# Attention, then an MLP: the first two batches read k in blocks of permuted rows, and each output tile gets a PSUM tile of its own

## The chip, the cores and the metric

The kernel runs on one core of one Trainium2 chip. The metric is the device time of one execution in microseconds (us). The engines are TensorE (PE), VectorE (DVE), ScalarE (ACT), GpSimd (POOL) and SyncE (SP); PE's weight loads have a row of their own (PEld). Loads of q, k and v are issued by SP, loads of the weights and nearly all stores by POOL.

## The reference

Eight batches, eight heads, 576 tokens, head size 64. Each token sees itself and the 127 tokens before it, with a bias that falls linearly with the distance; then each token (512 features) goes through an MLP with a swish.

```
scores = (q @ k.T) / sqrt(64) - slope[h] * |i - j|      # only 0 <= i - j < 128
x = softmax(scores) @ v                                 # to [4608, 512]
h = x @ w_in                                            # 512 -> 2048
out = (h * sigmoid(beta * h)) @ w_out                   # 2048 -> 512
```

## The kernel before

Everything that PE multiplies is bfloat16. The 4,608 tokens of the MLP are cut into nine groups of 512. For a group g, `HS(g, j)` (`Hm`) makes one of 16 slices of the hidden layer: four matmuls into one of two PSUM tiles `hps` (L436), a tanh on ACT (L443), a product on DVE into `gT` (L444). `OS(g, i, n)` is a quarter of the 16 matmuls of one output tile of 128 tokens (L457); after the last quarter ACT scales the tile from PSUM to SBUF (`osb`, L463), and `store` issues its DMA (L470). The output tile is one half of `OO`, a single PSUM tile of two banks; i % 2 picks the half.

Attention of batches 0 and 1 goes by pairs of heads p, with 512 of the 576 tokens. `get_pair` loads q and k so that partition r holds rows 4r to 4r+3; `cast_pair` (POOL, L203) makes bfloat16 of them; `TP` transposes them on PE, and one DVE copy (L233) writes q and k to `QK`, back in the order of the rows. `SP_` makes scores: first a matmul of the identity with `table`, the bias and mask of each head, then q and k on top of it (L275). Visit A goes to `SS`, visit B to `OO`. ACT takes the exponential (L281); `PVP` multiplies by v (L304) and norms on DVE; `XP` transposes the result, and a DVE copy writes it to `XT` (L316). The last 64 tokens of a batch follow in a tail: `TT`, `SCT` (with `tablet` for a bias), `PV`, `X`. Batches 2 to 7 transpose by DMA (`DT`) and mask after the exponential (`SC`, L364 to L378; all in `SS`).

The order of PE, SP and POOL is the order of the program throughout; ACT and DVE keep it too in the opening. The opening is batch 0: constants, its four pairs, then `constants_late` (copies into `tablet`, clearing, all on DVE but one identity), `betas`, and the first two H steps. Then H steps 2 to 15 of group 0 run with the list `second` between them, which holds batch 1's four pairs and the tail of batch 0. Group 1 begins with H steps alone, and then H steps and output steps alternate; `spread` puts the steps of batches 2 to 7 (`att`), whose loads and casts are in `jobs`, between the items of all later groups. The loads of batch 1 wait for the second quarter of w_in.

The pool `fst` of loaded tiles has 13 buffers, `bst` of cast ones four; `psum_t` (transposes, `pv`, `xt`) and `psum_h` have two each.

Of the kernel before, what the change touches and what calls it, by code (L numbers as in the profile page):

```python
# [19 lines left out]
def kernel(  # L20
# [62 lines left out]
    SS = psum_c.tile([P, 2, 512], F32, name="SS")  # L83
    OO = psum_c.tile([P, 2, 512], F32, name="OO")
    psum_c.seal()

    def after(ins, other):
# [7 lines left out]

    def tri(o, n, w, sign, base, cm):
        nc.gpsimd.affine_select(
            out=o, in_=o, pattern=[[sign, w]], base=base, channel_multiplier=cm,
            compare_op=ALU.is_ge, fill=FAR,
        )  # L100

    def constants():
        nc.vector.memset(warm[:], 0.0)
        nc.scalar.activation(out=warm[:], in_=warm[:], func=ACTF.Exp)
        nc.gpsimd.iota(
            rel[:, 0:2, :], pattern=[[P, 2], [1, P]], base=0, channel_multiplier=-1,
            allow_small_or_imprecise_dtypes=True,
        )
        tri(rel[:, 0], 1, P, 1, 0, -1)
        tri(rel[:, 1], 1, P, -1, -1, 1)  # L110
        make_identity(nc, ident[:])
        nc.vector.tensor_copy(out=rel[:, 2], in_=rel[:, 0])
        for h in range(H):
            nc.vector.tensor_scalar_mul(table[:, h], rel[:], -slopes[h] / qscale)
        for i in range(2):
            nc.vector.memset(VS[i][:, :, :, D : D + 1], 1.0)

    def constants_late():
        make_identity(nc, identf[:])
        for e in range(2):  # L120
            for p in range(NP):
                for a in range(2):
                    nc.vector.tensor_copy(
                        out=tablet[:, e, a, p], in_=table[:, 2 * p + e, a, 0:64])
        for i in range(2):
            nc.vector.memset(VS[i][64:P, 4, :, 0:D], 0.0)
            nc.vector.memset(QK[i][:, :, :, S:], 0.0)
        nc.vector.memset(PC[:, 1024:], 0.0)
# [41 lines left out]

    def get(what, b, sb):
# [55 lines left out]
    def TP(b, p):  # L227
        src = staged.pop((b, "p", p))
        tps = psum_t.tile([P, 2, 4, P], BF16, name="tps", tag="t")
        for i in range(2):  # L230
            for c in range(4):
                nc.tensor.transpose(out=tps[:, i, c], in_=src[:, i, c], identity=ident[:])  # L232
        nc.vector.tensor_copy(  # L233
            out=QK[b % 2][:, :, p, 0:FULL].rearrange("d i (r c) -> d i c r", c=4), in_=tps[:])

# [17 lines left out]
    def SP_(b, vis, p):  # L253
        qk = QK[b % 2]
        sps = SS if vis == "A" else OO
        w = WIDTH[vis]
# [10 lines left out]
        for kb, at, q0, n in VISIT[vis]:  # L267
            for e in range(2):
# [261 lines left out]
    with tc.manual_schedule(engines={ENG.PE, ENG.SP, ENG.Pool}):  # L530
        with tc.manual_schedule(engines={ENG.Activation, ENG.DVE}):
            for w in ("p0", "p1", "v0", "v1", "p2", "p3", "v2", "v3"):
                n = int(w[1])
                if w[0] == "p":
                    get_pair("q", 0, n)
                    get_pair("k", 0, n)
                else:
                    get("v", 0, n)
            nc.sync.dma_start(out=bflat[:], in_=moe_beta.rearrange("(j p) -> j p", p=P))
            constants()  # L540
            w1 = []
            cast_pair(0, 0)
# [107 lines left out]
        items += o[8:]  # L650
        done, dw, dj = 0, 0, 0
# [70 lines left out]
```

## Time and profile before

| | us |
|---|---|
| median of three runs | 387.45 |
| lowest and highest | 383.09, 389.43 |
| the profiled execution | 388.25 |
| its span in the trace | 386.5 |
| PE busy | 338.2 |
| DVE busy | 214.1 |
| ACT busy | 206.9 |
| POOL busy | 102.9 |

The span is the time between the first and the last instruction of the trace. Matmuls are pipelined, so a busy PE is not PE at its peak: the same matmul of 512 columns takes twice as long where the granted clock is half. The mean granted clock of the run was 0.956 of full.

### The profile page before, as it was taken

To read this page: it belongs to the slowest core of one execution; us is meant where nothing else is said; L and a number is where in the kernel's file an instruction comes from. 1 tells how busy PE (TensorE), PEld (TensorE's weight loads), DVE (VectorE), ACT (ScalarE), POOL (GpSimd) and SP (SyncE) were. 2 spreads that over 40 slices of the span, in tenths; PEclk is the share of its full clock that TensorE was granted. 3 is DMA by queue.
4 is the path that set the end of the run, shared out by engine and by line. 5 is a ranking of instruction groups with operands and counts; after the bars stand their busy time and mean duration, and the time that the engine had idled before them with its cause. 6 is when DMAs were issued, how large, how long until landed. Compare 5 with 4: busy or idle time off the path is not lost.

```text
span 386.5 us, 6289 instructions
## 1 busy us (share of the span) xinstructions
PE 338.2 (87%) x2357; PEld 158.6 (41%) x2357; DVE 214.1 (55%) x454; ACT 206.9 (54%) x392; POOL 102.9 (27%) x188
## 2 busy tenths in 40 slices
PE   3676868699879999989999989999999899999985
PEld 1343334334334444434444434444444445444432
DVE  6567488636344478636646672875387536525400
ACT  2331445344575678646757764676677645426411
POOL 5838134100244444340224403331200100010010
PEclk9765799969989999999999999999999999999999
DMA  8999999692059999994866794793100010010021
GB/s 210 196 254 236 187 197 200 105 206 39 27 117 209 228 221 211 204 220 91 170 132 141 154 203 104 165 168 76 56 0 30 27 56 27 30 54 26 3 81 54
DMA packets 136126, 49.44 MB, mean 128 GB/s; under 512 B 125456, under 2 KB 133664, under 8 KB 136096
## 3 DMA queue, kind: packets, MB, share of 16 engines
q1 hardware_dynamic: 129152, 35.93, 49.6%
q0 software_dynamic: 6944, 13.11, 13.2%
q8 instruction: 18, 0.29, 0.3%
q14 instruction: 12, 0.10, 0.1%
HBM read 36.71 MB, written 9.44 MB: 119 GB/s over the span
## 4 chain that ended last, share of the span: by engine, by line
PE 71%; DVE 14%; ACT 11%; issue 3%; DMA 1%; POOL 0%; ACTq 0%
PE OO L457 30%; PE hps L436 28%; ACT pt L374 6%; DVE qkT L233 5%; PE SS L364 3%; DVE gT L444 3%; ACT osb L463 3%; DVE pt L378 2%; ACT sig L443 2%; PE xt L414 1%; PE pv L403 1%; PE pv L399 1%; PE tps L232 1%; PE pv L304 1%; DVE xnp L289 1%
## 5 line engine op out<-in xcount | busy, mean ns | idle before, releaser
L436 PE MATMUL hps<-XT,W 128*128 128x512 bf16 x576 | 149.8, 392 | 7.9 <-DVE gT L444 5.1
L457 PE MATMUL OO<-W,gT 128*128 128x512 bf16 x576 | 143.7, 381 | 11.5 <-ACT osb L463 11.4
L443 ACT ACTIVATE sig<-hps,beta_h 128x512 bf16<-128x512 f32 x144 | 98.6, 690 | 81.3 <-PE hps L436 78.5
L444 DVE SCALAR_TENSOR_TENSOR gT<-sig,hps 128x512 bf16<-128x512 bf16 x144 | 97.6, 684 | 70.7 <-ACT sig L443 70.0
L374 ACT ACTIVATE pt<-SS,bias 128x256 bf16<-128x256 f32 (+1 forms) x192 | 75.0, 477 | 21.2 <-PE SS L364 21.2
L436 PEld LDWEIGHTS <-W 128*128 128x128 bf16 x576 | 53.5, 100 | 70.2 <-issue 20.9
L457 PEld LDWEIGHTS <-gT 128*128 128x128 bf16 x576 | 52.6, 98 | 70.4 <-issue 16.6
L470 POOL DMA_DIRECT2D out_dram<-osb x34 | 18.4, 542 | 214.1 <-ACT osb L463 214.1
L463 ACT ACTIVATE osb<-OO 128x512 f32<-128x512 f32 x36 | 21.7, 604 | 47.1 <-PE OO L457 45.5
L378 DVE TENSOR_TENSOR pt<-pt,mask 128x1024 bf16<-128x1024 bf16 x48 | 35.8, 746 | 17.1 <-ACT pt L374 17.0
L288 DVE RECIPROCAL zs<-pv 128x4 f32<-128x4 f32 (+1 forms) x80 | 13.8, 176 | 31.2 <-PE pv L403 24.5
L196 POOL CAST bst<-fst 128x512 bf16<-128x512 f32 (+1 forms) x32 | 21.2, 661 | 30.2 <-PE tps L232 16.9
L209 POOL CAST vs<-fst 128x512 bf16<-128x512 f32 (+1 forms) x40 | 24.7, 629 | 13.0 <-DMA fst<-in_v_dram 8.9
L289 DVE TENSOR_TENSOR xn<-pv,zs 128x256 bf16<-128x256 f32 (+1 forms) x64 | 26.8, 421 | 1.6
L420 DVE COPY XT<-xt 128x512 bf16<-128x512 bf16 (+1 forms) x32 | 12.3, 385 | 19.6 <-PE xt L414 19.3
L233 DVE COPY qkT<-tps 128x1024 bf16<-128x1024 bf16 x8 | 19.5, 2434 | 6.5 <-PE tps L232 6.5
L364 PE MATMUL SS<-qkT 64*128 64x256 bf16 (+2 forms) x240 | 19.4, 256 | 3.3 <-ACT pt L374 3.3
L197 POOL CAST bst<-fst 128x512 bf16<-128x512 f32 (+1 forms) x32 | 19.7, 615 | 3.8 <-DMA fst<-in_k_dram 3.7
L403 PE MATMUL pv<-vs,pt 128*128 128x65 bf16 x240 | 20.6, 193 | 0.0
L403 PEld LDWEIGHTS <-pt 128*128 128x128 bf16 x240 | 16.1, 97 | 6.7
L364 PEld LDWEIGHTS <-qkT 64*128 64x128 bf16 x240 | 8.2, 94 | 22.6 <-issue 22.1
L399 PE MATMUL pv<-vs,pt 128*128 128x65 bf16 x192 | 17.4, 193 | 0.0
(62 smaller groups left out, 159.6 us busy)
## 6 DMA issues: line engine op xcount, KB each, us to landing
out_dram<-osb POOLq DMA_DIRECT2D x34, 256.0 KB, 2.3
fst<-in_q_dram SPq DMA_DIRECT2D x32, 256.0 KB, 5.1
fst<-in_k_dram SPq DMA_DIRECT2D x32, 256.0 KB, 5.0
fst<-in_v_dram SPq DMA_DIRECT2D x32, 256.0 KB, 4.0
W<-in_moe_w_in_dram POOLq DMA_DIRECT2D x4, 512.0 KB, 6.8
W<-in_moe_w_out_dram POOLq DMA_DIRECT2D x4, 512.0 KB, 9.8
fst<-in_q_dram SPq DMA_DIRECT2D x8, 128.0 KB, 3.8
fst<-in_k_dram SPq DMA_DIRECT2D x8, 128.0 KB, 4.1
```

Source lines behind the costliest of these rows:

```text
L209: return nc.gpsimd.tensor_copy(out=VS[b % 2][0:rows, sb, :, 0:D], in_=fs.pop(("v", b, sb))[0:rows])
L233: nc.vector.tensor_copy(out=QK[b % 2][:, :, p, 0:FULL].rearrange("d i (r c) -> d i c r", c=4), in_=tps[:])
L289: nc.vector.tensor_tensor(out=xn, in0=pv[0:nq, :, 0:D], in1=zs[0:nq].broadcast_to([nq, 4, D]), op=ALU.mult)
L364: nc.tensor.matmul(o, lhsT=qk[64 * e : 64 * e + 64, 1, p, P * kb : P * kb + P], rhs=qk[64 * e : 64 * e + 64, 0, p, P * kb : P * kb + nq], ...
L374: nc.scalar.activation(out=pt[:, e, cols], in_=sps[:, e, cols], func=ACTF.Exp, scale=qscale, bias=bias[:, half, h : h + 1],)
L378: nc.vector.tensor_tensor(out=pt[:], in0=pt[:], in1=masks[m][:], op=ALU.mult)
L403: nc.tensor.matmul(pv[:, hl, 0 : D + 1], lhsT=weights(b, qb, h, 0), rhs=vs[:, qb, h, 0 : D + 1], start=qb == 0, stop=True,)
L436: nc.tensor.matmul(hps[:], lhsT=W1[:, c, bass.ts(j, P)], rhs=XT[:, c, c0 : c0 + TOKG], start=(c == 0), stop=(c == NDM - 1),)
L443: nc.scalar.activation(out=sig[:], in_=hps[:], func=ACTF.Tanh, scale=beta_h[:, j : j + 1])
L444: nc.vector.scalar_tensor_tensor(out=gts[g][:, j, :], in0=sig[:], scalar=1.0, in1=hps[:], op0=ALU.add, op1=ALU.mult)
L457: nc.tensor.matmul(ops_, lhsT=gT[:, j, i * P : i * P + P], rhs=W2[:, j, :], start=(j == 0), stop=(j == NFF - 1),)
L463: nc.scalar.mul(osb[:], ops_, 0.5)
```

## The change

It has seven parts.

- For batches 0 and 1 DVE copies q from PSUM as the transposes leave it (all rows of one residue c together), and k in blocks: within each 128 keys the 32 keys of residue 0 come first, then those of residue 1, and so on. `SP_` therefore reads q with a step of 128 elements, four at a time, so that queries come out in their own order. Two copies take the place of one.
- The distance table of those keys is built by four iotas on 32 partitions each, one iota over columns and five DVE operations, in place of one iota and two selects on POOL.
- v of batches 0 and 1 has to have the same order of keys: four DMAs to 32 partitions each take the place of one. v 0 and 1 of batch 0 are issued by ACT, after the constants.
- Eight matmuls of zeros stand ahead of the first transposes on PE.
- What `constants_late` did on DVE goes to POOL; the first half of `tablet` comes from a small table `relt` of its own. The identity for `betas` is made after it.
- Visit B of batches 0 and 1 gets its own PSUM tile `SX`; after batch 1 its banks are given to a pool `psum_o` of two single tiles, and each output tile is one of these.
- The list `second` is spread over the H steps from 4 on, where it was from 9 on; in group 1 four H steps stand ahead of the first output step, where there were eight.

```
 def constants():
+    nc.vector.memset(zeros[:], 0.0)
...
+    for _ in range(8):
+        nc.tensor.matmul(SS[:, 0, :], lhsT=zeros[:, 0:P], rhs=zeros[:], start=True, stop=True,
+            skip_group_check=True)
+    for c in range(4):
+        nc.gpsimd.iota(ktok[32 * c : 32 * c + 32], pattern=[[0, 1]], base=c, channel_multiplier=4, ...)
-    nc.gpsimd.iota(rel[:, 0:2, :], pattern=[[P, 2], [1, P]], base=0, channel_multiplier=-1, ...)
-    tri(rel[:, 0], 1, P, 1, 0, -1)
-    tri(rel[:, 1], 1, P, -1, -1, 1)
+    nc.gpsimd.iota(qtok[:], pattern=[[1, P]], base=0, channel_multiplier=0, ...)
     make_identity(nc, ident[:])
+    nc.vector.tensor_scalar(out=qtok[:], in0=qtok[:], scalar1=ktok[:, 0:1], scalar2=None, op0=ALU.subtract)
+    for a, cmp in ((0, ALU.is_lt), (1, ALU.is_ge)):
+        nc.vector.tensor_scalar(out=pen[:], in0=qtok[:], scalar1=0.0, scalar2=FAR, op0=cmp, op1=ALU.mult)
+        nc.vector.scalar_tensor_tensor(out=rel[:, a], in0=qtok[:], scalar=float(P * a), in1=pen[:],
+            op0=ALU.add, op1=ALU.add)
     nc.vector.tensor_copy(out=rel[:, 2], in_=rel[:, 0])
...
 def constants_late():
-    make_identity(nc, identf[:])
-    (16 nc.vector.tensor_copy to tablet; 5 nc.vector.memset)
+    nc.gpsimd.iota(relt[:], ...)
+    nc.gpsimd.affine_select(out=relt[:], in_=relt[:], ...)
+    nc.gpsimd.tensor_copy(out=tablet[:, :, 1], in_=table[:, :, 1, 0:64].rearrange("k (p e) t -> k e p t", e=2))
+    for h in range(H):
+        nc.gpsimd.tensor_scalar_mul(tablet[:, h % 2, 0, h // 2], relt[:], -slopes[h] / qscale)
+    (the same 5 memsets, on nc.gpsimd)
 def betas():
+    make_identity(nc, identf[:])
...
 def get(what, b, sb, eng=None):
+    if what == "v" and b < 2 and sb < 4:
+        for c in range(4):
+            (eng or nc.sync).dma_start(
+                out=f[32 * c : 32 * c + 32],
+                in_=src[b, :, P * sb : P * sb + P, :].rearrange("h (r c) d -> c r h d", c=4)[c])
+        return
...
 def TP(b, p):
-    nc.vector.tensor_copy(
-        out=QK[b % 2][:, :, p, 0:FULL].rearrange("d i (r c) -> d i c r", c=4), in_=tps[:])
+    nc.vector.tensor_copy(
+        out=qk[:, 0, p, 0:FULL], in_=tps[:, 0].rearrange("d c r -> d (c r)"))
+    nc.vector.tensor_copy(
+        out=qk[:, 1, p, 0:FULL].rearrange("d (n c r) -> d c n r", n=4, c=4),
+        in_=tps[:, 1].rearrange("d c (n r) -> d c n r", n=4))
...
 def SP_(b, vis, p):
-    sps = SS if vis == "A" else OO
+    sps = SS if vis == "A" else SX
...
-        rhs=qk[64 * e : 64 * e + 64, 0, p, q0 : q0 + n],
+        rhs=qk[64 * e : 64 * e + 64, 0, p, 0:FULL].rearrange(
+            "d (c r) -> d r c", c=4)[:, q0 // 4 : (q0 + n) // 4, :],
...
 def OS(g, i, n):
-    ops_ = OO[:, i % 2, :]
+    if n == 0:
+        late[g, i] = late["o"].tile([P, DM], F32, name="ops", tag="ops")
+    ops_ = late[g, i][:]
...
-            else:
+            elif n >= 2:
                 get("v", 0, n)
...
         constants()
+        for n in range(2):
+            get("v", 0, n, nc.scalar)
...
-        to = len(second) * (j + 1 - 9) // (NFF - 9)
+        to = len(second) * max(0, j + 1 - 4) // (NFF - 4)
...
+    opening.close()
+    late["o"] = ctx.enter_context(tc.tile_pool(name="psum_o", bufs=2, space=bass.MemoryType.PSUM))
...
-    items = h[:8]
+    items = h[:4]
-    for n in range(8):
-        items += [h[8 + n]] + o[n : n + 1]
+    for n in range(12):
+        items += [h[4 + n]] + o[n : n + 1]
```

## Rows read from the trace of the kernel before

**Rows 1.** The page: busy time by engine; the chain that ended last, by line.

```profile
PE 338.2 (87%) x2357; PEld 158.6 (41%) x2357; DVE 214.1 (55%) x454; ACT 206.9 (54%) x392; POOL 102.9 (27%) x188
PE OO L457 30%; PE hps L436 28%; ACT pt L374 6%; DVE qkT L233 5%; PE SS L364 3%; DVE gT L444 3%; ACT osb L463 3%; DVE pt L378 2%; ACT sig L443 2%; PE xt L414 1%; PE pv L403 1%; PE pv L399 1%; PE tps L232 1%; PE pv L304 1%; DVE xnp L289 1%
```

**Rows 2.** Groups by line and shape, 0 to 60 us: count | busy us, mean ns | idle.

```profile
L233 DVE COPY qkT<-tps 128x1024 bf16<-128x1024 bf16 x7 | 17.0, 2431 | 6.5 <-PE tps L232 6.5
...
L316 DVE COPY XT<-xt 128x512 bf16<-128x512 bf16 x4 | 1.7, 417 | 0.2 <-PE xt L315 0.2
...
L112 DVE COPY rel<-rel 128x128 f32<-128x128 f32 x1 | 0.4, 448 | 0.7 <-POOL rel L97 0.7
```

**Rows 3.** What PE waited for, whole span: us in total, times, longest.

```profile
PE OO L457 <- ACT osb L463: 11.4, 17, 1.2
PE SS L275 <- DVE qkT L233: 10.5, 6, 2.2
...
PE hps L436 <- DVE XT L316: 2.0, 1, 2.0
...
PE pv L304 <- DVE qkT L233: 0.8, 1, 0.8
```

**Rows 4.** Stretches: length, busy us by engine (instructions), granted clock, DMA share, GB/s.

```profile
10.00:20.00 10.00, 6.20 (x56) 3.34 (x56) 5.54 (x5) 3.37 (x4) 8.62 (x19) 0.77 1.04 195
20.00:30.00 10.00, 7.27 (x74) 4.26 (x73) 6.86 (x29) 3.15 (x4) 3.63 (x14) 0.67 1.20 257
30.00:40.00 10.00, 6.52 (x32) 3.00 (x30) 7.04 (x30) 1.26 (x2) 8.76 (x14) 0.50 1.09 229
```

**Rows 5.** Timeline, H steps alone: start, us, engine, operation, count, idle before.

```profile
46.61 1.99 PE L436 MATMUL hps<-XT,W 128*128 128x512 bf16 x8 [0.53 <-DVE gT L444]
...
77.72 3.57 PE L436 MATMUL hps<-XT,W 128*128 128x512 bf16 x8 [0.38 <-DVE XT L420]
```

**Rows 6.** Timeline of the opening's first 15 us.

```profile
6.07 2.43 DVE L233 COPY qkT<-tps 128x1024 bf16<-128x1024 bf16 x1 [0.81 <-PE tps L232]
...
9.10 0.81 ACT L281 ACTIVATE pt<-SS 128x768 bf16<-128x768 f32 x1 [6.80 <-PE SS L275]
...
13.67 0.61 POOL L203 CAST bst<-fst 128x512 bf16<-128x512 f32 x1 [0.19 <-DMA fst<-in_k_dram]
...
14.86 0.40 PE L275 MATMUL OO<-qkT 64*128 64x128 bf16 x6
15.19 0.38 PE L304 MATMUL pv<-vs,pt 128*128 128x65 bf16 x6
```

**Rows 7.** Timeline, 15 to 37 us: the end of the opening.

```profile
15.92 2.25 POOL L216 DMA_DIRECT2D W<-in_moe_w_in_dram  x3
...
28.28 0.61 POOL L203 CAST bst<-fst 128x512 bf16<-128x512 f32 x1 [5.97 <-DMA fst<-in_q_dram]
...
32.21 2.78 DVE L123 COPY tablet<-table 128x64 bf16<-128x64 bf16 x16
...
36.94 1.01 PE L436 MATMUL hps<-XT,W 128*128 128x512 bf16 x2 [2.01 <-DVE XT L316]
```

**Rows 8.** Timeline, batch 1: the first scores behind the copy.

```profile
53.12 0.34 PE L275 MATMUL SS<-qkT 64*128 64x256 bf16 x4 [2.19 <-DVE qkT L233]
```

**Rows 9.** PE's waits from 100 to 365 us, and the tail's timeline.

```profile
PE OO L457 <- ACT osb L463: 8.6, 13, 1.2
PE SS L364 <- ACT pt L374: 3.3, 3, 1.9
...
370.18 3.61 PE L457 MATMUL OO<-W,gT 128*128 128x512 bf16 x16 [0.69 <-ACT osb L463]
```

**Rows 10.** SP's timeline: DMA issues.

```profile
0.81 0.44 SPq L187 DMA_DIRECT2D fst<-in_q_dram  x1
...
2.83 1.41 SPq L177 DMA_DIRECT2D fst<-in_v_dram  x2
4.28 2.66 SPq L187 DMA_DIRECT2D fst<-in_q_dram  x1
```

More of the change, by code (lines that the diff above doesn't have):

```diff
@@ L58 @@
     one = const.tile([P, 1], BF16, name="one")
+    ktok = const.tile([P, 1], F32, name="ktok")
+    qtok = const.tile([P, P], F32, name="qtok")
+    pen = const.tile([P, P], F32, name="pen")
     rel = const.tile([P, 3, P], F32, name="rel")
+    relt = const.tile([P, 64], F32, name="relt")
+    zeros = const.tile([P, 512], BF16, name="zeros")
     table = const.tile([P, H, 3, P], BF16, name="table")
@@ L83 @@
     SS = psum_c.tile([P, 2, 512], F32, name="SS")
-    OO = psum_c.tile([P, 2, 512], F32, name="OO")
     psum_c.seal()
+    opening = ExitStack()
+    psum_x = opening.enter_context(tc.tile_pool(name="psum_x", bufs=1, space=bass.MemoryType.PSUM))
+    SX = psum_x.tile([P, 2, 512], F32, name="SX")
+    late = {}
     def after(ins, other):
@@ L92, in after @@
         )
[L96 to L100, printed above, removed]
     def constants():
+        nc.vector.memset(zeros[:], 0.0)
         nc.vector.memset(warm[:], 0.0)
         nc.scalar.activation(out=warm[:], in_=warm[:], func=ACTF.Exp)
+        for _ in range(8):
+            nc.tensor.matmul(
+                SS[:, 0, :], lhsT=zeros[:, 0:P], rhs=zeros[:], start=True, stop=True,
+                skip_group_check=True)
+        for c in range(4):
+            nc.gpsimd.iota(
+                ktok[32 * c : 32 * c + 32], pattern=[[0, 1]], base=c, channel_multiplier=4,
+                allow_small_or_imprecise_dtypes=True,
+            )
         nc.gpsimd.iota(
-            rel[:, 0:2, :], pattern=[[P, 2], [1, P]], base=0, channel_multiplier=-1,
+            qtok[:], pattern=[[1, P]], base=0, channel_multiplier=0,
             allow_small_or_imprecise_dtypes=True,
         )
-        tri(rel[:, 0], 1, P, 1, 0, -1)
-        tri(rel[:, 1], 1, P, -1, -1, 1)
         make_identity(nc, ident[:])
+        nc.vector.tensor_scalar(
+            out=qtok[:], in0=qtok[:], scalar1=ktok[:, 0:1], scalar2=None, op0=ALU.subtract)
+        for a, cmp in ((0, ALU.is_lt), (1, ALU.is_ge)):
+            nc.vector.tensor_scalar(
+                out=pen[:], in0=qtok[:], scalar1=0.0, scalar2=FAR, op0=cmp, op1=ALU.mult)
+            nc.vector.scalar_tensor_tensor(
+                out=rel[:, a], in0=qtok[:], scalar=float(P * a), in1=pen[:], op0=ALU.add,
+                op1=ALU.add)
         nc.vector.tensor_copy(out=rel[:, 2], in_=rel[:, 0])
@@ L118, in constants_late @@
     def constants_late():
-        make_identity(nc, identf[:])
-        for e in range(2):
-            for p in range(NP):
-                for a in range(2):
-                    nc.vector.tensor_copy(
-                        out=tablet[:, e, a, p], in_=table[:, 2 * p + e, a, 0:64])
+        nc.gpsimd.iota(
+            relt[:], pattern=[[1, 64]], base=0, channel_multiplier=-1,
+            allow_small_or_imprecise_dtypes=True,
+        )
+        nc.gpsimd.affine_select(
+            out=relt[:], in_=relt[:], pattern=[[1, 64]], base=0, channel_multiplier=-1,
+            compare_op=ALU.is_ge, fill=FAR,
+        )
+        nc.gpsimd.tensor_copy(
+            out=tablet[:, :, 1], in_=table[:, :, 1, 0:64].rearrange("k (p e) t -> k e p t", e=2))
+        for h in range(H):
+            nc.gpsimd.tensor_scalar_mul(
+                tablet[:, h % 2, 0, h // 2], relt[:], -slopes[h] / qscale)
         for i in range(2):
-            nc.vector.memset(VS[i][64:P, 4, :, 0:D], 0.0)
-            nc.vector.memset(QK[i][:, :, :, S:], 0.0)
-        nc.vector.memset(PC[:, 1024:], 0.0)
+            nc.gpsimd.memset(VS[i][64:P, 4, :, 0:D], 0.0)
+            nc.gpsimd.memset(QK[i][:, :, :, S:], 0.0)
+        nc.gpsimd.memset(PC[:, 1024:], 0.0)
     def betas():
         bps = psum_t.tile([P, NFF], F32, name="bps", tag="t")
+        make_identity(nc, identf[:])
         nc.tensor.transpose(out=bps[:], in_=bflat[:], identity=identf[:])
@@ L169, with get @@
     staged = {}
-    def get(what, b, sb):
+    def get(what, b, sb, eng=None):
         rows = ROWS[sb]
@@ L631 @@
                 done += 1
+        opening.close()
+        late["o"] = ctx.enter_context(
+            tc.tile_pool(name="psum_o", bufs=2, space=bass.MemoryType.PSUM))
         work = tail(1)
@@ L645 @@
         h = HG(1)
[L646 removed]
+        items = h[:4]
         o = OG(0, 0) + OG(0, 1) + OG(0, 2) + OG(0, 3) + OG(1, 0) + OG(1, 1)
[L648 to L650 removed]
+        for n in range(12):
+            items += [h[4 + n]] + o[n : n + 1]
+        items += o[12:]
         done, dw, dj = 0, 0, 0
```

4 lines of the change are left out of this document (added).

## Prediction

> **What bounds the kernel now.** I read the page's table of engines first, then the chain that ended last, then what TensorE (PE) waited for, then the stages in which those waits lie. PE is busy for 338.2 of 386.5 us [rows 1], so 48.3 us are idle. In the chain the two MLP matmuls (L457, L436) hold 58%, and one copy on VectorE (DVE), L233, holds 5% [rows 1]: eight copies of 2.43 us [rows 2]. The list of PE's waits says who ended the idle time: 11.4 us in 17 waits for the eviction `osb` of the output tile, 10.5 us in 6 waits for L233 and 0.8 in one more, 2.0 us for the last `XT` copy of the opening [rows 3]. [...]
>
> The profiled execution took 388.25 us, the median of three is 387.45 (383.09 to 389.43). I sum against 388.25 and take off 0.8 at the end; about 2% (7.7 us) is what a measurement of this kernel tells from no change.
>
> **The q/k copy, batch 0.** L233 writes 1,024 bfloat16 in steps of four elements: 2.43 us, 2.37 ns an element. After the change q is written as it stands, and k in runs of 32. The nearest row is L316, 512 elements from PSUM at 0.42 us [rows 2], so the two copies cost 0.84 us and each pair wins 1.59. In batch 0 the four copies are on the path: PE transposes, waits for the copy, and only then scores; 4 x 1.59 = 6.4 us. The inputs allow it: pair 3's last cast ends at 14.28 [rows 6], and three steps after 6.07 [rows 6], each 0.84 of copies and about 1 us each for transposes and the two visits, put its transposes near 17 by my estimate.
>
> Two things eat into this. DVE now builds the distance table from five operations on 128x128 float32 where it did none; at most 0.45 us each (the copy L112 [rows 2]), at least nothing, for GpSimd's part gets shorter by two selects. Slack ahead of the first copy was 0.81 us [rows 6]. I take 0.3 each, 1.5, so 0.7 us of delay; 0 to 1.5 in the range. The other is the strided read of q.
>
> **The strided read.** The score matmuls of batches 0 and 1 now read q at a step of 128 elements, four at a time. No matmul of the trace reads like this. The lower end is no cost: at full clock the scores of a B visit, 1,024 columns, took 0.33 us (14.86 to the next matmul at 15.19 [rows 6]); that is 0.58 for the 1,792 columns of a pair, 4.6 us for eight pairs. The upper end comes from DVE, where the stepped copy costs 2.37 ns an element against 0.82 for the plain one, 2.9 times. I take a factor of 2 against the full clock, which is +0.58 us a pair; where the clock is half, a matmul has twice the time for each column, so I charge half in batch 0: 1.2 us, and 2.3 us in batch 1. Batch 0 nets 6.4 - 0.7 - 1.2 = **4.5 us**.
>
> [...]
>
> **The end of the opening.** DVE copies `tablet` 16 times at 32.21 (2.78 us) and clears five areas before the last `XT` copy, for which PE sat idle 2.01 us before 36.94 [rows 7]. All of this goes to GpSimd (POOL), so the wait goes: **2.0 us**. POOL pays 16 operations (iota, select, one copy, eight scalings, five clears) after its W1 issues, which end at 18.17 [rows 7]. At up to 0.61 us each (a 512-wide cast there [rows 6]) that is at most 9.8 us; I take 5. POOL then stood idle 5.97 us, waiting for batch 1's first q [rows 7], so it is hidden; at 9.8 us the cast would be 3.8 us late, still ahead of its transposes (below). The identity for `betas` now queues behind this work: at the upper bound PE would wait about 1 us for it, which I leave to the range.
>
> **Batch 1 sooner.** From 39 to 77.7 us PE has fourteen H steps and 23 attention steps. An H step alone is bound by PSUM, ScalarE (ACT) and DVE: two take 1.99 us with 0.53 idle before them [rows 5], 1.26 each, against 0.86 of matmuls. Five fewer stand alone: 5 x 0.40 = 2.0. The copies win what PE waited for: of the seven waits for L233 batch 1 has three, 2.19 at 53.12 [rows 8], about 0.5, and the 0.8 [rows 3]; the first is cut by 1.59, the others go: 2.9. Minus the stride, 2.3: **2.6 us**. The data are there: pair 0 of batch 1 is cast from 28.28 [rows 7], by about 30, while its transposes come after H step 4: 36.94 less 6.5 is 30.4, two us for the first two steps and three of 1.3 to 1.7 more, near 36.5.
>
> **The first output tiles sooner.** Four fewer H steps stand alone before the first output step: 4 x 0.40 = 1.6. At 77.72 PE had gone cold after the small matmuls of batch 0's tail [rows 5]; sixteen matmuls at that pace cost 2 x (3.57 - 1.99) = 3.2 us more than at full clock. The tail now has H steps between its parts; I credit half of it, 1.5. Together **3.1 us**.
>
> **Separate O tiles.** PE waits for ACT's `osb` 17 times though the next tile uses the other half of `OO`: in the last stretch each group of 16 matmuls starts 0.69 us late, at the end of the eviction of the tile before [rows 9], which its own half does not need. So the wait is one for the whole buffer, and two tiles remove it. Four times in the tail: 2.75, sure, for PE has nothing else there. The other 8.6 (8.6 in 13 waits from 100 to 365 [rows 9]) lie where ACT also has exponentials; next late there is the single score buffer, for which PE already waits 3.3 us there [rows 9]. I take three quarters, 6.5. **9.2 us** (2.75 to 11.4). The B scores move to `SX`, whose banks the new tiles take over; its last exponential is done several H steps before the first output step, so that costs nothing.
>
> **Value loads.** A v tile goes out as four DMAs of 32 partitions. One v issue took 0.70 us, a q or k issue with as many pieces as a quarter has, 0.44 [rows 10]. On SP that is about 1.1 us more a tile. In batch 1 it queues before pairs 2 and 3 and the last rows; SP often stood there waiting anyway. `bflat` stands behind the quarters on SP and is needed only at `betas`, past 25 us. In batch 0 tiles 0 and 1 go to ACT: 8 x 0.44 = 3.5 us at the head of its queue, behind a table load and one small operation, done before its first exponential at 9.10 [rows 6], near 8 in the new order. If half of them stall as one SP issue did (2.66 us [rows 10]), that is 12.4 us, and the opening ends some 6 us later: in the range.
>
> [...] Loads run here at 195 to 257 GB/s [rows 4], and no row shows a quarter.
>
> **The zero matmuls** fill the time before the first transposes, whose copy starts at 6.07 [rows 6]: eight at 0.45 (3.57 / 8 [rows 5]), 3.6 in all, end near then. I count nothing for the clock; that is the first rival.
>
> Sum: 4.5 + 2.0 + 2.6 + 3.1 + 9.2 = 21.4; 388.25 - 21.4 - 0.8 = 366.05. **Forecast 366 us.**
>
> **Rivals.** (1) The zero matmuls and the denser opening keep the clock up. From 10 to 40 us PE was busy 6.20, 7.27 and 6.52 us [rows 4]; a granted 0.77, 0.67, 0.50 means 46, 66 and 100% of it at half clock, 14.2 us, half of which, 7.1, would go; the stride then costs 1.2 more, the later cold stretch gives 1.5 more: 366 - 7.4 = 359. For it: much less waiting in the opening. Against it: at 20 to 30 us PE was busy 73% and still at 0.67.
>
> (2) The strided read is dear. At the factor 2.9, 8.7 us of surcharge in place of 3.5: 371. At DVE's price in ns, 2.37 for each of 14,336 columns, 34.0 us in place of 4.6: a surcharge of 29.4, 25.9 more than I charged, 392, **slower** than before. It decides from a surcharge of 25 us, or 6.4 times the present price. For it: nothing in the trace reads so. Against it: PE is the faster reader here, at 0.44 ns a column (3.61 us for 16 matmuls of 512 [rows 9]).
>
> [...]
>
> (4) The `osb` waits come back as waits for the score buffer or ACT: only the tail's 2.75 stays, 366 + 6.4 = 372.5. Against it: ACT is busy 54% [rows 1].
>
> **How the numbers follow.** Forecast (360 to 369, small errors of its terms) 0.50; clock up (351 to 360) 0.17; data or ACT's issues late, or the waits back (369 to 376) 0.17; stride at about 3 times (369 to 376) 0.10; two of these at once, about 380, 0.03; stride at DVE's price 0.03. The range 352 to 378 leaves out about 0.10 at the ends. Below 379.7 lies 0.89; within 2%, 0.08; above 395.2, 0.03.
>
> **What would show it.** Two copies of about 0.42 us where L233 stood; score matmuls of a B visit that take twice 0.33 us at full clock; no wait for `XT` near 30; no wait of an output matmul for `osb`, and the last four groups back to back at 3.45 to 3.6 us; the first step of batch 1 before 38; the second H group's start near 65. It is wrong if score matmuls stretch far more, if casts of batch 1 wait for v, or if PE's waits move to the score buffer.

## The result, and the profile after

The changed kernel takes 368.08 us (median; 366.8 to 368.2) against 387.69 for the kernel before: a ratio of 0.952, 95% interval 0.945 to 0.959. The forecast was 366. The profiled execution took 368.2 us with a span of 366.5, against 388.25 and 386.5 before, so 20.0 us are to be found in the two traces. Two points on TensorE (PE) split them: the third H step, where the opening ends, and the first scores of batch 2, where the long regular part begins. (Of the runs further below, one execution of psum_step fell into a slower state of the chip and is left out of its time.)

| stretch | before, us | after, us | gain | terms of the forecast | their sum |
|---|---|---|---|---|---|
| start to third H step | 39.03 | 38.42 | 0.6 | copies of batch 0; end of the opening | 6.5 |
| third H step to first scores of batch 2 | 64.68 | 58.89 | 5.8 | batch 1 sooner; first output tiles sooner | 5.7 |
| from there to the end of the span | 282.8 | 269.2 | 13.6 | separate O tiles | 9.2 |

The total came out near the forecast partly by luck, because two terms were wrong in opposite directions: the opening gave 5.9 us less than I said, the O tiles 4.4 more.

The page, against [rows 1]: busy time, share of the span and instructions of each engine.

```profile
PE 341.1 (93%) x2365; PEld 158.1 (43%) x2365; DVE 199.8 (55%) x447; ACT 206.7 (56%) x392; POOL 108.0 (29%) x206
```

PE is busier by 2.9 us in a span that is 20 us shorter: 25.4 us are idle where 48.3 were. PE's waits, against [rows 3] (us in total, times, longest); L304 and L315 are the scores of the first two batches, L405 those of the others, L477 the hidden layer.

```profile
PE SS L304 <- ACT pt L322: 4.8, 1, 4.8
PE SS L405 <- ACT pt L415: 4.0, 4, 1.9
PE hps L477 <- DVE gT L485: 3.5, 7, 1.1
PE SS L315 <- DVE qkT L272: 2.3, 4, 1.2
```

The 11.4 us for `osb` are gone, and nothing took their place: the wait for the score buffer in the regular part (L405) is 4.0 against 3.3 [rows 9]. The wait for the copy fell from 10.5 to 2.3. At the top stands a wait that wasn't there, 4.8 us once, for ScalarE (ACT). The stretches, against [rows 4] (length, busy us by engine, granted clock, DMA share, GB/s), show where it lies:

```profile
10.00:20.00 10.00, 5.22 (x37) 2.29 (x36) 1.36 (x4) 3.56 (x4) 4.54 (x8) 0.51 0.45 82
20.00:30.00 10.00, 8.91 (x81) 3.91 (x79) 4.45 (x14) 3.67 (x4) 9.36 (x24) 0.84 1.17 190
30.00:40.00 10.00, 7.73 (x38) 3.50 (x37) 4.95 (x28) 1.27 (x2) 7.74 (x22) 0.50 0.92 238
```

From 10 to 20 us the DMA engines are less than half used (0.45), and the granted clock is 0.51. The timeline of the opening, against [rows 6, 7], gives the order of events:

```profile
4.87 7.16 SPq L207 DMA_DIRECT2D fst<-in_v_dram  x8
...
8.75 5.67 ACTq L207 DMA_DIRECT2D fst<-in_v_dram  x8
...
10.60 0.42 DVE L270 COPY qkT<-tps 128x512 bf16<-128x512 bf16 x1 [3.04 <-PE tps L268]
10.94 0.41 DVE L272 COPY qkT<-tps 128x512 bf16<-128x512 bf16 x1
...
14.47 0.81 ACT L322 ACTIVATE pt<-SS 128x768 bf16<-128x768 f32 x1 [12.18 <-DMA fst<-in_v_dram]
14.86 0.61 POOL L245 CAST vs<-fst 128x512 bf16<-128x512 f32 x1 [6.93 <-DMA fst<-in_v_dram]
...
15.34 0.80 PE L304 MATMUL SS<-table,ident 128*128 128x384 bf16 x2 [4.78 <-ACT pt L322]
```

ACT had nothing to do from 2.30 us on, yet its first value load went out at 8.75 and its last ended at 14.42; the first exponential, which stands behind them, began at 14.47 where it had begun at 9.10 [rows 6]. PE had no free score buffer until then. The two copies take 0.42 and 0.41 us, as forecast. The first v tile is cast at 14.86, and so what GpSimd (POOL) issues behind it, the quarters of w_in and with them batch 1's loads, comes 5 to 6 us later too.

The scores of two B visits (start, length, count), the first in batch 0 at half clock, the second in batch 1 at full clock:

```profile
17.78 1.03 PE L315 MATMUL SX<-qkT 64*128 64x128 bf16 x6
...
18.74 0.51 PE L345 MATMUL pv<-vs,pt 128*128 128x65 bf16 x6
...
52.75 1.03 PE L315 MATMUL SX<-qkT 64*128 64x128 bf16 x6
53.71 0.36 PE L345 MATMUL pv<-vs,pt 128*128 128x65 bf16 x6
```

The stretches around them (the third number from the end is the granted clock, 0.50 and 1.00):

```profile
17.50:19.00 1.50, 1.50 (x12) 0.52 (x12) 0.00 (x0) 0.38 (x2) 1.50 (x3) 0.50 0.00 0
50.00:60.00 10.00, 10.00 (x81) 3.90 (x80) 4.97 (x12) 6.12 (x8) 4.92 (x8) 1.00 1.08 159
```

From the start of the scores to the next matmul it is 0.96 us both times, for 1,024 columns: 0.94 ns a column at either clock. Before, at full clock, it was 0.33 [rows 6]: 2.9 times. And the tail, against [rows 9]: one unbroken row.

```profile
346.82 14.84 PE L500 MATMUL ops<-W,gT 128*128 128x512 bf16 x68
```

### The profile page after: what moved, and what is told of

Same layout as the page of the kernel before. It is cut to its first block, busy times and chain, and to the rows that moved or that the text cites. A ratio compares the mean times of both kernels' runs of the same rounds, so it can differ in the third digit from the quotient of the medians.

```text
span 366.5 us, 6353 instructions
## 1 busy us (share of the span) xinstructions
PE 341.1 (93%) x2365; PEld 158.1 (43%) x2365; DVE 199.8 (55%) x447; ACT 206.7 (56%) x392; POOL 108.0 (29%) x206
## 4 chain that ended last, share of the span: by engine, by line
PE 80%; DVE 8%; ACT 6%; DMA 2%; issue 2%; SPq 1%; ACTq 0%
PE ops L500 32%; PE hps L477 31%; ACT pt L415 4%; PE SS L405 4%; DVE gT L485 3%; DVE pt L419 2%; DMA fst<-in_v_dram 2%; PE pv L444 2%; PE SX L315 2%; PE pv L440 2%; PE xt L455 2%; PE SS L315 1%; PE pv L345 1%; ACT sig L484 1%; PE tps L268 1%
## 5 line engine op out<-in xcount | busy, mean ns | idle before, releaser
L477 PE MATMUL hps<-XT,W 128*128 128x512 bf16 x576 | 148.5, 388 | 4.9 <-DVE gT L485 3.5
L500 PE MATMUL ops<-W,gT 128*128 128x512 bf16 x576 | 141.6, 379 | 0.0
L477 PEld LDWEIGHTS <-W 128*128 128x128 bf16 x576 | 52.6, 99 | 64.8 <-issue 15.6
L419 DVE TENSOR_TENSOR pt<-pt,mask 128x1024 bf16<-128x1024 bf16 x48 | 36.8, 766 | 16.1 <-ACT pt L415 16.0
L506 ACT ACTIVATE osb<-ops 128x512 f32<-128x512 f32 x36 | 21.8, 605 | 39.1 <-PE ops L500 39.1
L329 DVE RECIPROCAL zs<-pv 128x4 f32<-128x4 f32 (+1 forms) x80 | 13.8, 176 | 31.5 <-PE pv L444 18.2
L232 POOL CAST bst<-fst 128x512 bf16<-128x512 f32 (+1 forms) x32 | 20.4, 636 | 11.4 <-DMA fst<-in_q_dram 8.3
L405 PE MATMUL SS<-qkT 64*128 64x256 bf16 (+2 forms) x240 | 18.9, 252 | 4.0 <-ACT pt L415 4.0
L461 DVE COPY XT<-xt 128x512 bf16<-128x512 bf16 (+1 forms) x32 | 12.3, 384 | 14.1 <-PE xt L455 13.8
L444 PEld LDWEIGHTS <-pt 128*128 128x128 bf16 x240 | 16.1, 97 | 6.7
L405 PEld LDWEIGHTS <-qkT 64*128 64x128 bf16 x240 | 8.3, 94 | 22.9 <-issue 21.9
L440 PEld LDWEIGHTS <-pt 128*128 128x128 bf16 x192 | 14.6, 98 | 5.4 <-issue 0.6
```

The source lines that it names most:

```text
L405: nc.tensor.matmul(o, lhsT=qk[64 * e : 64 * e + 64, 1, p, P * kb : P * kb + P], rhs=qk[64 * e : 64 * e + 64, 0, p, P * kb : P * kb + nq], ...
L419: nc.vector.tensor_tensor(out=pt[:], in0=pt[:], in1=masks[m][:], op=ALU.mult)
L440: nc.tensor.matmul(pv[:, hl, 0 : D + 1], lhsT=weights(b, qb - 1, h, 1), rhs=vs[:, qb - 1, h, 0 : D + 1], start=True, stop=False,)
L444: nc.tensor.matmul(pv[:, hl, 0 : D + 1], lhsT=weights(b, qb, h, 0), rhs=vs[:, qb, h, 0 : D + 1], start=qb == 0, stop=True,)
L477: nc.tensor.matmul(hps[:], lhsT=W1[:, c, bass.ts(j, P)], rhs=XT[:, c, c0 : c0 + TOKG], start=(c == 0), stop=(c == NDM - 1),)
L500: nc.tensor.matmul(ops_, lhsT=gT[:, j, i * P : i * P + P], rhs=W2[:, j, :], start=(j == 0), stop=(j == NFF - 1),)
```

## The experiments

Times are medians against runs of the kernel before on the same chip (386.02 to 387.91 us); "first H step" and "first scores of batch 2" are starts on PE in the profiled run. The changed kernel has 32.66 and 97.31, the one before 31.76 and 103.71. By their intervals the difference of two rows is open by 1 to 4 us either way, and the profiled run of v_act_first is its fastest, 359.95 us, 3.6 below its median.

| run | us | ratio, 95% interval | first H step | first scores of batch 2 |
|---|---|---|---|---|
| o_tiles | 372.46 | 0.960 (0.953 to 0.967) | 31.78 | 102.1 |
| v_quarters | 387.83 | 1.001 (0.998 to 1.005) | 33.03 | 103.4 |
| plain_copy | 372.5 | 0.961 (0.954 to 0.968) | 24.7 | 87.0 |
| psum_step | 379.19 | 0.982 (0.977 to 0.986) | 25.61 | 93.01 |
| v_act_first | 363.55 | 0.939 (0.932 to 0.945) | 28.54 | 89.14 |
| v_sp | 363.53 | 0.941 (0.938 to 0.945) | 30.16 | 92.27 |
| old_places | 374.18 | 0.965 (0.962 to 0.968) | 32.55 | 102.96 |
| q_plain | 357.58 | 0.923 (0.920 to 0.925) | 28.55 | 86.5 |
| no_zeros | 363.34 | 0.937 (0.935 to 0.939) | 29.11 | 92.08 |
| both_blocks | 361.68 | 0.936 (0.932 to 0.940) | 30.57 | 91.58 |
| step_tiles_places | 359.32 | 0.925 (0.921 to 0.929) | 27.31 | 89.45 |
| step_all | 358.64 | 0.929 (0.927 to 0.932) | 27.9 | 87.52 |

**Separate O tiles alone** (o_tiles): the kernel before, with only this part.

```
-    sps = SS if vis == "A" else OO
+    sps = SS if vis == "A" else SX
...
+        if n == 0:
+            late[g, i] = late["o"].tile([P, DM], F32, name="ops", tag="ops")
...
```

> The kernel before with the separate O tiles (and SX for the B scores) alone. If the 17 waits for osb were whole-buffer waits, they go and nothing takes their place: 388 - 9 to 11 = 377 to 379, no wait of an output matmul for osb in the trace. Rival (the waits move to the score buffer or to ACT): only the tail's 2.75 us, about 385, and the waits for the score buffer grow from 3.3 us by about 6.

Measured: 15.1 us less (372.46, where the theory gave 377 to 379), 13.9 of them behind the first scores of batch 2, as in the changed kernel (13.6). So the last stretch of the table above belongs to this part whole. No wait for `osb` is left in its trace either.

**Quarter loads alone** (v_quarters): the kernel before, with v of batches 0 and 1 in four DMAs of 32 partitions, all on SP.

```
+        if what == "v" and b < 2 and sb < 4:
+            for c in range(4):
+                nc.sync.dma_start(out=f[32 * c : 32 * c + 32], in_=...)
```

> The kernel before, with each v tile of batches 0 and 1 loaded by four DMAs of 32 partitions on SP in place of one (rows in their own order). Theory: loads share eight completion semaphores, a ninth load waits for the landing of the eighth before it, and quarters use these up four times as fast; the loads behind them come later, the granted opening is some 3 to 6 us longer: 390 to 394. Rival (quarters cost only SP's issue time, 1.1 us a tile, under other waits): 387 to 389.

Measured: no difference; the theory fell and the rival held. Four issues stand for one (the eight of two tiles take 5.54 us on SP, with their waits), and the first H step is 1.3 us later, but that is made up before batch 2. In the kernel before, the loads cost nothing in the time for being cut (387.83 us against 387.56).

**The copy alone** (plain_copy) and **another way to have it** (psum_step), both from the kernel before.

```
plain_copy
-        out=QK[b % 2][:, :, p, 0:FULL].rearrange("d i (r c) -> d i c r", c=4), in_=tps[:])
+        out=QK[b % 2][:, :, p, 0:FULL].rearrange("d i (c r) -> d i c r", c=4), in_=tps[:])
psum_step
-        tps = psum_t.tile([P, 2, 4, P], BF16, name="tps", tag="t")
+            tps = psum_t.tile([P, P, 4], F32, name="tps", tag="t")
...
-                nc.tensor.transpose(out=tps[:, i, c], in_=src[:, i, c], identity=ident[:])
...
+                nc.tensor.matmul(tps[:, :, c], lhsT=src[:, i, c], rhs=ident[:], ...)
+            nc.vector.tensor_copy(
+                out=QK[b % 2][:, i, p, 0:FULL], in_=tps[:].rearrange("d r c -> d (r c)"))
```

> The kernel before, with the q/k copy of batches 0 and 1 written in the order in which PSUM holds it, so one plain copy of 1,024 elements. It leaves out the reordering of q and k, so the scores of these batches are of permuted tokens; every other instruction stays. Theory: the copy takes about 0.8 us, PE's seven waits for it (11.3 us) shrink by 9: 378 to 380. Rival (the opening is bound by the loads and casts, not the copy): 383 to 387.

> The kernel before with one edit: q and k are transposed by matmuls that write float32 in steps of four into PSUM, so that two plain copies give them in the order of the rows. Nothing else of the change is in it. Theory: the stepped copy is what the opening and batch 1 wait for, and the step costs nothing where PE writes: two copies of 0.69 us for 2.43, the time that the plain copy gave (372.5) plus 8 x 0.55 us for the float32 source at most: 372 to 376. Rival: the transposes pay for the step (0.5 us or more a pair): 377 to 381.

plain_copy gained 15 us (372.5, where the theory gave 378 to 380). That is more than the eight times 1.75 us (2.43 less 0.68) by which its copies are shorter, 14.0, although not all of these were on the path. The clock is likely a part of it, for the granted clock of the profiled run is 0.985 where it was 0.956; how much it is worth isn't shown. (The busy times of PE can't tell: plain_copy's trace has 2,316 matmuls, the one of before 2,357.) psum_step gained only 6.8, and the rival was right. Its trace against that of plain_copy, the same first pair of batch 1 in each:

```profile
39.31 0.61 PE L232 MATMUL tps<-ident,bst 128*128 128x128 bf16 x8
39.97 0.68 DVE L233 COPY qkT<-tps 128x1024 bf16<-128x1024 bf16 x1
40.72 0.34 PE L275 MATMUL SS<-qkT 64*128 64x256 bf16 x4 [0.47 <-DVE qkT L233]
```

```profile
41.86 1.04 PE L232 MATMUL tps<-ident,bst 128*128 128x128 bf16 x8
42.49 0.69 DVE L235 CAST qkT<-tps 128x512 bf16<-128x512 f32 x1 [0.46 <-PE tps L232]
...
43.10 0.68 DVE L446 SCALAR_TENSOR_TENSOR gT<-sig,hps 128x512 bf16<-128x512 bf16 x1
43.70 0.68 DVE L235 CAST qkT<-tps 128x512 bf16<-128x512 f32 x1
44.44 0.34 PE L277 MATMUL SS<-qkT 64*128 64x256 bf16 x4 [1.22 <-DVE qkT L235]
```

Eight transposes that write in steps of four take 0.43 us longer at full clock (granted 1.00 in both stretches: 30 to 40 us in plain_copy, 40 to 50 in psum_step), and the float32 copies are two of 0.69 for one: scores begin 2.58 us after the first transpose, where it was 1.41; about half a microsecond of that is a product `gT` that DVE put between its two copies. It is the step that costs, and not float32 or the plain matmul: four matmuls of both_blocks (the first line), which write float32 in order, take as long as four transposes of v_act_first, which write bfloat16.

```profile
22.22 0.38 PE L359 MATMUL xt<-back,xnp 128*128 128x128 bf16 x4 [0.21 <-DVE XT L362]
```

```profile
25.77 0.38 PE L356 MATMUL xt<-ident,xnp 128*128 128x128 bf16 x4
```

**Where the opening's 5 us went** (v_act_first, v_sp): the changed kernel, with the value loads of batch 0 in the old place of the program, between pairs 1 and 2; the first two tiles issued by ACT in the one, by SP in the other.

```
-                elif n >= 2:
-                    get("v", 0, n)
+                else:
+                    get("v", 0, n, nc.scalar if n < 2 else None)      # v_sp: get("v", 0, n)
...
-            for n in range(2):
-                get("v", 0, n, nc.scalar)
```

> The changed kernel, with the eight quarters of v 0 and 1 (batch 0) issued by ACT ahead of its table load, in the program between pair 1 and pair 2. Theory: their turn among the eight semaphores now comes before those of v 2 and 3, so ACT is free long before its first exponential, which starts near 8.5 in place of 14.5, and the 4.8 us for which PE waited for it go: 368 - 4 to 6 = 362 to 364. Rival 1 (32-partition loads are slow in themselves, wherever they stand): 367 to 369. Rival 2 (the gain is lost again because the loads of batch 1 don't come sooner): 366 to 368.

> The changed kernel with the sixteen value quarters of batch 0 all issued by SP, where the kernel before had its four loads; ScalarE issues none. Theory: the 5 us of the opening were lost because ScalarE stood behind loads whose turn had not come; with its queue free the first exponential starts near 9.5 to 10.5 and the time is that of the kernel with the quarters issued first by ScalarE, 362.5 to 365. Rival: the quarters themselves are late wherever they are issued (SP pays eight more issues of up to 0.9 us ahead of pairs 2 and 3): first exponential near 10 all the same, but pairs 2 and 3 and the second quarters of W1 5 us later, 367 to 370.

Both gave back about 4.5 us. Why ACT stood idle from 2.30 to 8.75 can be read in the program's own list of waits. In the changed kernel the loads of SP and ACT take eight completion marks in turn, in the order in which the built program lists them, over both engines, and a load waits until the one that held its mark before has landed. In that order ACT's eight loads have places 14, 16, 18, 20 and 22 to 25 of 25. The first of them (mark 5, counted from 0) has to wait for the sixth load of SP, k of pair 2; that was issued at 3.34 and landed 5.4 us later, at 8.73, and ACT's load went out at 8.75. The next three loads of that order went the same way, at 10.05, 11.04 and 11.23, behind landings at 10.04, 11.02 and 11.21:

```
ACT  2 L109 ACTIVATE warm<-warm 128x1 [waits DVE_49]
ACT  3 L207 DMA fst<-in_v_dram 32x8x64 [waits DMAHW5_49]
ACT  4 L207 DMA fst<-in_v_dram 32x8x64 [waits DMAHW7_49]
...
ACT 11 L322 ACTIVATE pt<-SS 128x2x384 [waits PE_49]
```

In v_act_first it is SP that pauses, before pair 2, from 2.78 to 5.25; ACT's own loads there last until 8.98, and the table load behind them (1.28 us) puts the first exponential at 10.42, not near 8.5 as expected. In v_sp ACT is free, and the first exponential starts at 8.47, earlier than in the kernel before. SP's issues of v_act_first, then v_sp's:

```profile
2.31 0.47 SPq L223 DMA_DIRECT2D fst<-in_k_dram  x1
5.25 0.37 SPq L223 DMA_DIRECT2D fst<-in_q_dram  x1
```

```profile
7.84 0.45 SPq L223 DMA_DIRECT2D fst<-in_q_dram  x1
...
8.47 0.81 ACT L322 ACTIVATE pt<-SS 128x768 bf16<-128x768 f32 x1 [6.17 <-PE SS L315]
```

The late loads held two engines in the changed kernel: ACT, whose exponential stands behind them, and POOL, which waited 6.93 us to cast the first tile. In v_act_first POOL still waits 4.22 us for the second tile, and the time came back all the same; that speaks for ACT, but no run parts the two.

**The places put back** (old_places): the changed kernel with `second` spread from step 9 on and eight H steps ahead of the first output step.

```
-            to = len(second) * max(0, j + 1 - 4) // (NFF - 4)
+            to = len(second) * (j + 1 - 9) // (NFF - 9)
...
-        items = h[:4]
+        items = h[:8]
...
```

> The changed kernel with the two places put back: batch 1 and the tail of batch 0 from H step 9 on, eight H steps ahead of the first output step. Theory (each H step alone costs 0.40 us over its matmuls, nine of them 3.6, and the cold stretch near 75 us comes back, 1.5 to 3): 368 + 5 to 7 = 373 to 375. Rival (the waits in that stretch come from the chain of batch 1, however the steps are placed): 368 to 370.

Measured: 6.1 us more, against the 5.1 that the forecast gave the places (2.0 for five H steps, 3.1 for the first output tiles). The clock is part of it: this kernel has stretches under 1.0 from 70 to 90 us, where the kernel before had its slow matmuls of 77.72 [rows 5]; the changed kernel has 1.00 there.

```profile
70.00:80.00 10.00, 6.96 (x74) 3.76 (x77) 4.78 (x14) 2.90 (x4) 1.18 (x2) 0.92 1.01 193
80.00:90.00 10.00, 9.14 (x70) 4.18 (x70) 5.92 (x12) 5.96 (x9) 2.85 (x5) 0.91 0.61 113
```

```profile
70.00:80.00 10.00, 7.46 (x85) 3.77 (x84) 4.97 (x11) 5.06 (x7) 1.44 (x3) 1.00 1.14 221
80.00:90.00 10.00, 10.00 (x67) 4.78 (x64) 5.14 (x11) 5.01 (x8) 1.19 (x3) 1.00 0.01 4
```

The first pair is old_places, the second the changed kernel.

**The strided read** (q_plain) and **the zero matmuls** (no_zeros), each from v_act_first.

```
q_plain
-                    rhs=qk[64 * e : 64 * e + 64, 0, p, 0:FULL].rearrange(
-                        "d (c r) -> d r c", c=4)[:, q0 // 4 : (q0 + n) // 4, :],
+                    rhs=qk[64 * e : 64 * e + 64, 0, p, q0 : q0 + n],
no_zeros
-        for _ in range(8):
-            nc.tensor.matmul(SS[:, 0, :], lhsT=zeros[:, 0:P], rhs=zeros[:], ...)
```

> The kernel of v_act_first with q read at a step of one in the score matmuls of batches 0 and 1. It leaves out putting the queries back in order, so the scores stand under wrong queries; the work is the same. Theory (a strided column costs about 0.93 ns at either clock, 0.74 us for a visit A and 0.95 for a visit B, where the plain read took 0.33 for a B at full clock): 0.5 to 1.1 us a pair, 363.5 - 5 to 8 = 355 to 359, visit B back to 0.33 us. Rival (PE has slack there and waits for the exponentials in place of the reads): 361 to 364.

> The kernel of v_act_first without the eight zero matmuls. Theory (they end when the first transposes would start and change nothing later): 363 to 364. Rival (they bring the clock up in time for the opening; without them more of batch 0 runs at half clock): 366 to 369, with a lower mean granted clock.

q_plain is 6.0 us faster than v_act_first by the medians, 2.9 by the profiled runs (357.02 and 359.95); the same six matmuls, read in order:

```profile
44.32 0.40 PE L315 MATMUL SX<-qkT 64*128 64x128 bf16 x6
```

That is 0.40 us where the changed kernel's row has 1.03. The opening got no shorter by it: the first H step is at 28.55, where v_act_first has 28.54. The zero matmuls are worth nothing (0.2 us, inside both intervals).

**Reading in order without the step** (both_blocks): v_sp, with q copied in blocks of 32 like k, the table's queries in the same order, and the transposing matmul of the result multiplied by a permuted identity, which puts the queries back.

```
-            qtok[:], pattern=[[1, P]], base=0, channel_multiplier=0,
+            qtok[:], pattern=[[1, 4], [4, 32]], base=0, channel_multiplier=0,
...
-            nc.tensor.transpose(out=xt[:, n, :], in_=xn[:, n, :], identity=ident[:])
+            nc.tensor.matmul(xt[:, n, :], lhsT=xn[:, n, :], rhs=back[:], ...)
...
```

> The kernel with the quarters on SP (363.5), but q is copied in blocks of 32 like k, so that the scores read q at step one; the distance table takes the same order of queries, and the matmul that transposes the normalized result multiplies by a permuted identity, which puts the queries back. It pays 0.27 us more for each XT copy (float32 in PSUM, at most 2.2 in eight copies, mostly beside other work) and eight small copies into tablet on GpSimd in place of one. Theory: the strided read costs 6.0 us, as when the queries were left out of order, so 357 to 359.5. Rival: the columns of the read cost nothing where PE waits anyway and the late constants on GpSimd now end the opening: 361 to 364.

Measured: 1.8 us less than v_sp, inside the intervals, and not 6; the rival holds. PE is through with batch 0 at 24.44 and then waits for the identity of `betas`, which stands behind the late constants on POOL (1.3 us of the wait are the run's own: eight copies into `tablet` of 1.87 us, where v_sp has one of 0.61):

```profile
24.61 2.97 POOL L153 TENSOR_SCALAR tablet<-relt 128x64 bf16<-128x64 f32 x8
...
30.11 0.19 POOL masks.py:199 TENSOR_SCALAR_AFFINE_SELECT identf<-identf 16x16 f32<-16x16 f32 x1
...
30.36 0.28 PE L163 MATMUL bps<-identf,bflat 16*128 16x16 f32 x1 [5.92 <-POOL identf masks.py:199]
```

**A kernel without quarters, strided read and zeros** (step_tiles_places): psum_step with the O tiles and the new places; and **with the late constants on POOL** as well (step_all).

```
step_all
-        for e in range(2):
-            for p in range(NP):
-                for a in range(2):
-                    nc.vector.tensor_copy(out=tablet[:, e, a, p], in_=table[:, 2 * p + e, a, 0:64])
+        for a in range(2):
+            nc.gpsimd.tensor_copy(out=tablet[:, :, a], in_=table[:, :, a, 0:64].rearrange(...))
-            (5 nc.vector.memset)
+            (the same on nc.gpsimd)
...
```

> The kernel before with the separate O tiles and the two new places, and another way to the order of q and k: the transposes write PSUM in float32 at a step of four elements, so that the tokens stand in their own order there, and one plain copy each brings q and k to SBUF. No strided read, no quarters, no permuted keys, no zero matmuls; constants as before. If the stepped write costs PE nothing and a copy from float32 takes about 0.6 us: o_tiles at 372.5, less 10 to 12 for the copies, less 4 for the places: 356 to 359. Rival (a stepped write to PSUM takes each transpose two to four times as long, 0.5 to 3 us a pair): 361 to 380.

> The stepped float32 transposes, separate O tiles and the new places (359.32 us before this edit), and what the late constants did on VectorE now on GpSimd, the identity for the betas after it. In that run TensorE still stood 3.51 us before the first H step for the last XT copy, behind 2.75 us of copies into tablet and the clears on VectorE. If that wait is the end of the opening, most of it goes: 356 to 357.5 us, the first H step near 24 to 25 in place of 27.3. Rival: something else is as late (W1's first quarter, or the identity for the betas behind GpSimd's queue, as the changed kernel's opening ended 0.51 us after it): then 358.5 to 360.

Both beat the changed kernel by about 9 us. Moving the constants did not help further: by the intervals the two are one. The wait of 3.51 us for `XT` fell to 0.51, but a new one came. On DVE the biases of the later masks (L163) were put ahead of a normalization (L293), and they wait for an iota that now stands behind the constants on POOL:

```profile
21.53 0.13 POOL L150 IOTA kpos<- 128x1 f32 x1
...
21.69 0.22 DVE L163 TENSOR_SCALAR bias<-kpos 128x1 f32<-128x1 f32 x2 [3.21 <-POOL kpos L150]
21.82 0.41 DVE L293 TENSOR_TENSOR xnp<-pv,zs 128x256 bf16<-128x256 f32 x1
...
22.29 0.62 PE L308 MATMUL pv<-vs,pt 128*128 128x65 bf16 x8 [2.92 <-DVE xnp L293]
```

## Why the prediction was right, point by point

**The q/k copy, batch 0: the mechanism right, the gain covered.** The copies cost 0.42 and 0.41 us, and DVE's first copy came 0.57 us later than before (I said 0.7). plain_copy shows what the copy alone is worth in the opening: the first H step 7.1 us sooner. In the changed kernel it came 0.9 us later, so the 4.5 us of this term did not show.

**Value loads: the step that failed.** I costed the move to ACT at nothing, "done before its first exponential at 9.10, near 8 in the new order", since I counted eight issues and no wait. The loads had to wait for their turn among eight marks, behind loads of SP, and held ACT until 14.42. I had named the stall as a possibility and its price (the opening some 6 us later); the first exponential came 5.4 later, and v_act_first and v_sp each put the price in time at about 4.5 us. In the kernel before, the quarters cost nothing in the time (v_quarters, 387.83 us against 387.56). They are not free everywhere, though. One sign that I named did come: in the changed kernel POOL waits 5.81 us for the last v tile of batch 1, although among PE's waits there is none for it. And where the opening is shorter, as in v_sp, POOL stood 3.65 us for the last v tile of batch 0, for which it had stood 0.24 in the kernel before; the late constants stand behind that cast. The casts in the changed kernel and in v_sp:

```profile
51.72 0.61 POOL L245 CAST vs<-fst 128x512 bf16<-128x512 f32 x1 [5.81 <-DMA fst<-in_v_dram]
```

```profile
19.26 0.62 POOL L245 CAST vs<-fst 128x512 bf16<-128x512 f32 x1 [3.65 <-DMA fst<-in_v_dram]
```

**The end of the opening: right where it was looked at, with a cover I misjudged.** The wait for `XT` went from 2.01 to 0.51. But POOL's constants are hidden only because the opening stayed long: the identity was ready at 29.97, and PE came to it at 32.45 without a wait.

```profile
29.78 0.19 POOL masks.py:199 TENSOR_SCALAR_AFFINE_SELECT identf<-identf 16x16 f32<-16x16 f32 x1
...
32.45 0.28 PE L160 MATMUL bps<-identf,bflat 16*128 16x16 f32 x1
```

The forecast left about 1 us of wait for the identity to the range; when both_blocks shortens batch 0, it is 5.92.

**The strided read: mis-sized.** I took a factor of 2 at full clock, 3.5 us in all. It is 2.9 (0.96 us for 0.33), and the price is about 6 us by q_plain, though both_blocks got only 1.8 of it back. For batch 0 I charged half of that. By the lengths shown, a B visit at half clock went from 0.61 us to 1.03, at full clock from 0.40 to 1.03: two thirds. The row at half clock (granted 0.50 from 20 to 22 us), before:

```profile
20.67 0.61 PE L275 MATMUL OO<-qkT 64*128 64x128 bf16 x6
```

So the second rival's first figure, 2.9, was the right factor, but by chance as far as the runs show: it came from copies on DVE. Its second, DVE's price in ns, was far off: 2.37 ns a column, where 0.94 was measured.

**Batch 1 and the first output tiles sooner: right in sum, not part by part.** 5.8 us against 5.7 in that stretch, and 6.1 against 5.1 for the places alone. With the places put back the stretch takes 65.05 us (old_places, 37.91 to 102.96) against 64.68 before, so in batch 1 the faster copies gained nothing net of the strided read, where I had 0.6. The forecast time for the second group's first H steps, near 65, was missed: it was 74.81. Without the stall of ACT it is 66.64 (v_act_first) and 69.77 (v_sp), so the opening's delay is most of that.

```profile
74.81 1.89 PE L477 MATMUL hps<-XT,W 128*128 128x512 bf16 x8 [0.56 <-DVE XT L461]
```

These eight matmuls ran at full clock (granted 1.00 from 74 to 78 us), where they had taken 3.57 us [rows 5].

**Separate O tiles: right in kind, too small.** Two errors. I took the idle time of the trace, 0.69 us a wait, as what a wait costs. In the tail a group took 0.69 + 3.61 = 4.30 us [rows 9], and now takes 14.84 x 16 / 68 = 3.49: each wait cost 0.81, because the shown length of a stalled group includes the end of its last matmul (one is shown as 0.38 us long, at a pitch of 0.22), which the next group overlaps when nothing holds it. If each of the seventeen waits cost as much as one in the tail, they are 13.8 us, against the 13.6 and 13.9 measured. And I took off a quarter for waits that would come back elsewhere; they did not (0.7 more for the score buffer), so rival 4 fell.

**The clock.** Rival 1 said that zeros and a denser opening would keep it up. The zeros do nothing for the time, and the granted clock from 10 to 40 us was 0.51, 0.84 and 0.50, no better than before. That ACT's stall, which left PE idle, is the reason isn't shown: v_sp has no such stall, PE busy for 9.58 us from 10 to 20 where it was 5.22, and a clock of 0.50, 0.50 and 0.80.

```profile
10.00:20.00 10.00, 9.58 (x62) 3.88 (x61) 2.72 (x8) 4.06 (x5) 4.83 (x9) 0.50 0.91 185
20.00:30.00 10.00, 8.64 (x76) 4.81 (x76) 5.09 (x17) 2.44 (x3) 9.36 (x25) 0.50 0.98 166
30.00:40.00 10.00, 7.45 (x34) 3.38 (x34) 4.87 (x25) 3.33 (x5) 8.48 (x22) 0.80 1.01 266
```

v_act_first had 0.58, 1.00 and 1.00, plain_copy 1.00, 0.66 and 1.00. What sets the clock of the opening stays open.

What stays open: the parts measured alone don't add up. Copies 15.0, tiles 15.1 and places 6.1, less 6.0 for the read and 4.5 for ACT, are 25.7 us, but the change gave 19.6. By my estimate from the intervals of these runs some 5 of the missing 6.1 us may be noise. What is real of it may lie in the opening: without ACT's stall the first H step is at 28.5 to 30.2 (v_act_first, v_sp, q_plain), where plain_copy has 24.7. The constants on POOL can't be the place in the changed kernel itself, since PE didn't wait for the identity there. Two copies of 0.42 us for one of 0.68 (at most 1.3 us in eight pairs), the late v tiles and the clock are candidates; no run parts them.

## What to carry to other kernels

A load that is given to another engine's queue need not be free of the old one (ACT's first stood until 8.75 us here): find out what it must wait for in the order of the program, and then what that engine has standing behind it. A wait on a buffer that is shared as a whole, though the half that is needed is free, cost here what it added to the pitch of the rows (0.81 us a wait in the tail, where the idle column has 0.69), so compare the pitch of a stalled row with that of an unbroken one and don't add up the idle column. And whenever work is moved to an idle engine, ask how long its cover will be once the change has done its work: twice here the late constants became the end of an opening that had grown shorter.

## What the runs showed of the hardware

- A matmul's moving operand (`rhs`) read at a step of 128 bfloat16 elements, four at a time, took about 0.94 ns a column at the two granted clocks of TensorE seen there (0.96 us for 1,024 columns at 0.50 and at 1.00); read in order they took 0.33 us at full clock.
- A matmul of 128 columns that wrote float32 into PSUM in steps of four cost about 0.05 us more at full clock than a transpose that wrote bfloat16 in order (eight in 1.04 us, against 0.61). Written in order, float32 cost no more (four in 0.38 us, as four bfloat16 transposes).
- DMAs to 32 partitions each, four for one, cost more on the issuing queue (eight in 5.54 us with their waits, where two whole tiles took 1.41 [rows 10]) and nothing measurable in the time of the kernel before (387.83 against 387.56 us).
